# Splitting the remainder weights of a SwiGLU feed-forward part in batches during attention

## The chip, the core and the metric

The kernel runs on one core of a Trainium2 chip. A core has five engines with queues of their own: TensorE (PE, with its weight loads as PEld), VectorE (DVE), ScalarE (ACT), GpSimd (POOL) and SyncE (SP), which here only issues DMAs. ACT issues some DMAs too. Sixteen DMA engines serve all queues. The metric is the device time of one execution in microseconds (us); lower is better.

## What is computed

One transformer block with adaptive layer norm, over 2048 tokens of width 576, all in float32:

```python
mod = silu(c) @ w_mod                      # six rows: sa, ca, ga, sb, cb, gb
h = layernorm(x) * (1 + ca) + sa
x = x + ga * A(h)                          # infini-attention: 32 heads of 18, 4 segments of 512
h = layernorm(x) * (1 + cb) + sb
x = x + gb * ((silu(h @ w_gate) * (h @ w_up)) @ w_down)     # w_gate, w_up: 576 x 4608
```

Attention works segment by segment: softmax over the segment's own 512 keys, mixed with a read of a memory that earlier segments wrote.

## The kernel before

TensorE multiplies in a fast float32 form that drops low bits. To keep precision, an operand is split in two: a high part (ACT casts it) and a low part, the rest (DVE subtracts the high part from the operand). A product is then high x high, low x high and high x low.

**Attention** is one loop over 32 units (four segments with eight groups of four heads) of 11 steps each. In every unit, `p2_step` makes scores (line 599 on PE), their exponential (L602 on ACT) and a causal mask (L606 on POOL); `av_step` (L619) multiplies by the values; `p1_step` (L182, L187) finds the row maxima of a unit two ahead. A table of events (`PAT`) puts the other steps at fixed places of the unit: the output projection `wo_m` (L729) with its DVE addition `wo_x` (L734), the memory read, layer norms. From unit 17 on, `stage_a` and `stage_b` also make part of the feed-forward input; they use the tile `yh12` as scratch. Further work can be hung on step number 11u + k with `at(step, function)`. Each engine runs its instructions in the order in which this loop issues them.

**The feed-forward part** uses Strassen's scheme: seven products in place of eight for the gate and up projections. The features are worked in 18 pairs of blocks of 128 (`p`), each with a gate set and an up set (`z` = 0 and 1), 36 sets in all, and the tokens in two halves (`t`). A half of the width has 288 = 2 x 128 + 32 rows; the 2 x 128 go through the split weights `wh` and `wl` (made by `prep_w`, ACT L1164 and DVE L1165), and the 32 left over, the remainder, go through one product with a tile `wr` (`R[z]`) of 96 used partitions: high part, low part, high part in bands of 32 rows. Four of the seven weight combinations are loaded, three more and a replaced one are sums of these (`sum_o`, L1155). In the first half a set's weights are loaded (`load_o`, tile `O` of 3 x 128 columns, of which the third holds the remainder repeated four times), summed on POOL, and split. The remainder is split by `prep_r`: a cast on ACT (L1149) and a subtraction on DVE (L1150), in two parts of three and four combinations. `store_o` and `store_r` write sums and `wr` to DRAM on ACT's queue, and in the second half they are loaded from there instead.

A pair of blocks has 14 steps `k`; each is one of the seven products for one `z` (seven matmuls at L1200 into banks A, B or C, the last with `wr`), and the down projection of the previous pair lies between them (L1304, L1321). The place of every load, sum and split is written by hand as a condition on `k`. Splits run ahead of their product by `PF` = 5 steps.

Between attention and the first half stands a handover: the last output projections (32 pieces `n`, line 729) run on TensorE, while the first weight sets are loaded, summed (at `n` in `SS`) and split (at `n` in `WW`, DVE's share one piece later through `later` and `flush`) and the rest of the input `y` is made (`y_sum` L1037, `y_here` L1044 and L1046) or loaded (`load_y`, L1122).

Of the kernel before, what the change touches and what calls it, by code (L numbers as in the profile page):

```python
# [7 lines left out]
F32 = mybir.dt.float32  # L8
# [7 lines left out]
P = 128  # L16
# [47 lines left out]
LNA = 1  # L64
S1B, S2B, XB, WB = 2, 2, 2, 1
# [7 lines left out]
def block(ctx: ExitStack, tc: tile.TileContext, x, wqk, wv, wo, beta, wgu, wd, c, w_mod, out):  # L73
# [76 lines left out]
    rD = [[dr.tile([96, 7, P], F32, tag=f"rD{p}_{z}", name=f"rD{p}_{z}") for z in range(2)] for p in range(NF // 2)]  # L150
# [883 lines left out]

    def y_sum(kb):
        n = P if kb < 2 else 96
        nc.gpsimd.tensor_tensor(ys[:n, kb], yh(2, kb)[:n], yh(0, kb)[:n], op=ALU.subtract)  # L1037
# [94 lines left out]
    def load_o(t, p, z):  # L1132
        O[p, z] = o = opl.tile([P, 7, 3, P], F32, tag="O", name="O", bufs=2)
        if t == 0:
            nc.sync.dma_start(o[:, 0:4], wgu[p, z])
        else:
            nc.sync.dma_start(o[:, 0:3, 0:2], wgu[p, z][:, 0:3, 0:2])
            nc.sync.dma_start(o[:, 3:7, 0:2], oD[p][z])

    def store_o(p, z):  # L1140
        nc.scalar.dma_start(oD[p][z], O[p, z][:, 3:7, 0:2])

    def prep_r(t, p, z, part=0):
        r = R[z]
        if t == 1:
            (nc.sync if p or z == 0 else nc.scalar).dma_start(f32(r[0:96]), rD[p][z])
            return
        o, c = O[p, z], slice(0, 3) if part == 0 else slice(3, 7)
        nc.scalar.copy(r[0:96, c], o[0:96, c, 2, :])  # L1149
        later.append(lambda: nc.vector.tensor_tensor(r[32:64, c], o[32:64, c, 2, :], f32(r[32:64, c]), op=ALU.subtract))  # L1150

    def sum_o(p, z, j, eng=nc.gpsimd):
        o = O[p, z]
        d, a, b, op = ((4, 3, 2, ALU.add), (5, 4, 0, ALU.subtract), (3, 0, 3, ALU.subtract), (6, 1, 5, ALU.subtract))[j]
        eng.tensor_tensor(o[:, d], o[:, a], o[:, b], op=op)  # L1155

    def store_r(p, z):
        nc.scalar.dma_start(rD[p][z], f32(R[z][0:96]))

    def prep_w(p, z, m):  # L1160
        o = O[p, z][:, SLOT[m], 0:2]
# [178 lines left out]
    with tc.manual_schedule():  # L1340
# [5 lines left out]
        for u in range(NU + 1):  # L1346
# [38 lines left out]
        load_o(0, 0, 1)  # L1385
        load_y(0, 1)
# [13 lines left out]
        for i in range(4):  # L1400
            for h in range(2):
                for c in range(WC):
# [42 lines left out]
        for t in range(2):  # L1445
            for p in range(NPR):
# [16 lines left out]
                for k in range(14):  # L1463
# [130 lines left out]
def _pairs(*ws):  # L1594
# [5 lines left out]
    r = w[..., 256:, :]  # L1600
    w = np.concatenate([w[..., :256, :], r, r, r, r], axis=-2)
    w = w.reshape(n, len(ws), 2, 2, 3, P, P).transpose(0, 1, 5, 2, 3, 4, 6)
    return np.stack([w[:, :, :, 0, 0], w[:, :, :, 0, 1], w[:, :, :, 1, 1], w[:, :, :, 1, 0]], axis=3)
# [31 lines left out]
```

## Time and profile before

| | |
|---|---|
| median of 3 runs | 1904.1 us (1901.33 to 1904.87) |
| the profiled execution | 1902.24 us |
| its span | 1900.5 us |
| granted TensorE clock, mean | 0.996 |
| instructions | 30716 |
| TensorE, DVE, ACT, POOL busy | 98%, 79%, 49%, 31% |
| DMA traffic | 304.31 MB |

The span runs from the first to the last instruction of the program. Attention runs from 256 to about 615 us of it, the first feed-forward half begins near 642.5 us, the second near 1276 us. In the profile's rows, "out<-in" are the program's tile names, and what stands in brackets is idle time of the engine just before and what ended it. A wait is put down to the engine whose signal came last.

### The profile page before, as it was taken

The numbers are of one execution on the slowest core, as the hardware profiler recorded it, in microseconds if no ns is written. First come the engines' busy times: TensorE is split into PE (matmuls) and PEld (weight loads), VectorE is DVE, ScalarE is ACT, GpSimd is POOL, SyncE is SP. The second block draws the span as 40 slices with busy tenths as digits, with TensorE's granted clock in tenths as the row PEclk, the third lists the DMA queues.
The fourth block names the chain that finished last, engine by engine and source line by source line (L and its number), as shares of the span: only waits on it lengthen the run. The fifth ranks groups of instructions, "written<-read, shape, count | busy, mean of one in ns | idle before, by whom it ended". The sixth has DMA issues, their size and how long they took to land.

```text
span 1900.5 us, 30716 instructions
## 1 busy us (share of the span) xinstructions
PE 1862.9 (98%) x10927; PEld 1559.2 (82%) x10927; DVE 1509.0 (79%) x3277; ACT 933.8 (49%) x2060; POOL 584.4 (31%) x789
## 2 busy tenths in 40 slices
PE   6999999999999899999999999999999999999999
PEld 4888866676766788888888888888888888888888
DVE  6566358878886688898898888876888888888887
ACT  1222267768767444445454454444445454454542
POOL 5212236555556555545544545400000000000000
PEclk9999999999999899999999999999999999999999
DMA  6767555446654854454454454378343233333331
GB/s 190 259 221 249 200 193 155 132 136 175 184 159 127 282 201 160 157 196 158 153 189 158 164 171 149 135 262 257 102 123 104 85 115 102 124 102 101 108 108 59
DMA packets 179424, 304.31 MB, mean 160 GB/s; under 512 B 26152, under 2 KB 107688, under 8 KB 177352
## 3 DMA queue, kind: packets, MB, share of 16 engines
q1 hardware_dynamic: 150696, 245.29, 40.9%
q10 hardware_dynamic: 28576, 57.07, 8.6%
q8 instruction: 86, 1.41, 0.3%
q14 instruction: 66, 0.54, 0.1%
HBM read 187.98 MB, written 113.77 MB: 159 GB/s over the span
## 4 chain that ended last, share of the span: by engine, by line
PE 90%; DVE 3%; DMA 2%; ACT 2%; POOL 1%; issue 1%; SPq 0%; ACTq 0%; DVEq 0%; POOLq 0%
PE A L1200 23%; PE pd L1321 13%; PE C L1200 12%; PE pd L1304 9%; PE B L1200 6%; PE pp L99 6%; PE s L599 4%; PE av L619 4%; PE s L182 4%; PE pv L99 2%; PE pw L729 2%; PE pn L800 1%; PE px L640 1%; ACT Pt L602 1%; PE pm L448 1%
## 5 line engine op out<-in xcount | busy, mean ns | idle before, releaser
L1200 PE MATMUL A<-y,wh 128*128 128x512 f32 x1152 | 404.5, 392 | 1.7 <-ACT B L1246 1.1
L187 DVE CUSTOM_DVE_ANT_0 junk<-s,tri 128x256 bf16<-128x256 f32 (+3 forms) x512 | 228.4, 486 | 68.4 <-PE s L182 60.9
L1165 DVE TENSOR_TENSOR wl<-O,wh 128x256 fp32r<-128x256 f32 x504 | 264.1, 529 | 3.3 <-ACT wh L1164 2.8
L1200 PEld LDWEIGHTS A<-y,wh 128*128 128x128 f32 x1152 | 216.7, 188 | 42.6 <-ACT B L1246 1.7
L1200 PE MATMUL A<-y,wl 128*128 128x512 f32 x576 | 224.8, 390 | 0.0
L602 ACT ACTIVATE Pt<-s 128x512 f32<-128x512 f32 (+1 forms) x352 | 187.9, 559 | 70.2 <-PE s L599 64.4
L1155 POOL TENSOR_TENSOR O<-O 128x384 f32<-128x384 f32 x140 | 158.1, 1142 | 174.3 <-DMA O<-in_wgu_dram 78.8
L1200 PE MATMUL C<-y,wh 128*128 128x512 f32 x576 | 203.6, 394 | 3.8 <-DMA y<-yD 2.5
L1309 DVE TENSOR_TENSOR acc<-acc,pd 128x576 f32<-128x576 f32 x216 | 162.2, 751 | 54.8 <-PE pd L1304 50.6
L1164 ACT CAST wh<-O 128x256 fp32r<-128x256 f32 x504 | 196.9, 405 | 0.8 <-issue 0.7
L1321 PE MATMUL pd<-dh,ah 128*128 128x288 f32 x640 | 189.8, 297 | 0.3 <-DVE acc L1325 0.3
L1321 PE MATMUL pd<-dh,al 128*128 128x288 f32 x640 | 188.2, 294 | 0.0
L1321 PE MATMUL pd<-dl,ah 128*128 128x288 f32 x640 | 188.1, 294 | 0.0
L1325 DVE TENSOR_TENSOR acc<-acc,pd 128x576 f32<-128x576 f32 x156 | 116.7, 749 | 81.8 <-PE pd L1321 81.7
L1264 ACT CAST ah<-sg 128x512 fp32r<-128x512 f32 x192 | 119.3, 621 | 86.1 <-DVE sg L1224 80.4
L599 PE MATMUL s<-qs,ks 110*128 110x512 f32 (+2 forms) x384 | 150.1, 407 | 2.9 <-ACT Pt L602 2.4
L182 PE MATMUL s<-ks,qs 108*128 108x256 f32 (+3 forms) x512 | 140.4, 327 | 1.9 <-DVE mx L187 1.8
L1265 DVE TENSOR_TENSOR al<-sg,ah 128x512 fp32r<-128x512 f32 x192 | 135.6, 707 | 7.1 <-ACT ah L1264 6.8
L1304 PE MATMUL pd<-dh,ah 128*128 128x288 f32 x448 | 132.9, 297 | 0.0
L1304 PE MATMUL pd<-dl,ah 128*128 128x288 f32 x448 | 131.9, 294 | 0.0
L1304 PE MATMUL pd<-dh,al 128*128 128x288 f32 x448 | 131.2, 293 | 0.0
L1200 PEld LDWEIGHTS C<-y,wh 128*128 128x128 f32 x576 | 108.1, 188 | 24.1 <-DMA y<-yD 2.9
(364 smaller groups left out, 4410.9 us busy)
## 6 DMA issues: line engine op xcount, KB each, us to landing
O<-in_wgu_dram SPq DMA_DIRECT2D x36, 768.0 KB
oD<-O ACTq DMA_DIRECT2D x36, 512.0 KB
O<-oD SPq DMA_DIRECT2D x36, 512.0 KB
ks<-kD SPq DMA_DIRECT2D x64, 216.0 KB
qs<-qD SPq DMA_DIRECT2D x64, 216.0 KB
O<-in_wgu_dram SPq DMA_DIRECT2D x36, 384.0 KB
rD<-wr ACTq DMA_DIRECT2D x36, 336.0 KB
wr<-rD SPq DMA_DIRECT2D x35, 336.0 KB
```

What stands on the lines that cost most here:

```text
L99: nc.tensor.matmul(ps, lhsT=a, rhs=b, start=(k == 0), stop=(k == 13))
L182: nc.tensor.matmul(bank[:, n * (h - h0):n * (h - h0) + n], lhsT=qst[b][0:108, h, 128 * i:128 * i + 128], rhs=kst[b][0:108, h // 2, 0:n], s ...
L187: nc.vector.tensor_tensor_reduce(junk[:, :n], bank[:, n * (h - h0):n * (h - h0) + n], tri[:, L - n:], 1.0, -3e38, op0=ALU.add, op1=ALU.max ...
L599: nc.tensor.matmul(bank[:, n * (g - h):n * (g - h + w)].rearrange("p (a b) -> p a b", a=w), lhsT=kst[u % NB][0:110, g // 2, 128 * j:128 * ...
L602: nc.scalar.activation(pt[:, h:h + per, :n], bank[:, :n * per].rearrange("p (a b) -> p a b", a=per), AF.Exp, scale=SCALE)
L1155: eng.tensor_tensor(o[:, d], o[:, a], o[:, b], op=op)
L1164: nc.scalar.copy(wh, o)
L1165: later.append(lambda: nc.vector.tensor_tensor(wl, o, f32(wh), op=ALU.subtract))
L1200: nc.tensor.matmul(bank, lhsT=a, rhs=b, start=(first and n == 0), stop=(n == 6), skip_group_check=not first)
L1304: nc.tensor.matmul(pd[:, i, :288], lhsT=a[:, tk], rhs=w, start=(k == 0), stop=(k == 2))
L1309: nc.vector.tensor_tensor(o, o, pd[:, :, :288], op=ALU.add)
L1321: nc.tensor.matmul(pd[:, i, :288], lhsT=a[:, tk], rhs=w, start=(k == 0), stop=(k == 5))
```

## The change

The remainders of all 36 weight sets are now split in one place, during attention, by a new function `stage_r`. It works in nine batches of four sets, a batch taking two units (22 steps), in units 0 to 17. The host lays the remainders out in a tensor `wgr` of their own, four sets on 4 x 32 = 128 partitions. A batch is: one load on SP (262 KB, 8 steps ahead), four sums on POOL of 128 columns (steps 3 to 6 of the even unit), four casts on ACT of 7 x 32 columns (steps 0 to 3 of the odd unit) with four subtractions on POOL one step later, and two stores on SP of 459 KB (step 8 of the odd unit): the high part and the low part. Scratch is `yh12`, from unit 0 on.

Both halves load `wr` with three DMAs of 32 partitions on SP, high, low, high: `load_r` at steps k = 2 and k = 9, where the second half had one DMA of 96 partitions. `prep_r` and `store_r` are gone. The tile `O` has 2 x 128 columns in place of 3 x 128, its load 512 KB in place of 768 KB in the first half, and `sum_o` 256 columns in place of 384.

```diff
+SUMS = ((4, 3, 2, ALU.add), (5, 4, 0, ALU.subtract), (3, 0, 3, ALU.subtract), (6, 1, 5, ALU.subtract))
...
-    rD = [[dr.tile([96, 7, P], F32, tag=f"rD{p}_{z}", name=f"rD{p}_{z}") for z in range(2)] for p in range(NF // 2)]
+    rD = [[dr.tile([P, 7, P], F32, tag=f"rD{b}_{i}", name=f"rD{b}_{i}") for i in range(2)] for b in range(NF // 4)]
...
+    def stage_r():
+        big = flat(yh12.rearrange("p a b c -> p (a b) c"))
+        ts = [big[:, 896 * i:896 * i + 896].rearrange("p (a b) -> p a b", b=P) for i in range(3)]
+        for b in range(NF // 4):
+            o, h, g = ts[b % 2], ts[2].bitcast(F32R), 22 * b
+            at(max(0, g - 8), lambda b=b, o=o: nc.sync.dma_start(o[:, 0:4], wgr[b]))
+            for j, (d, x_, y_, op) in enumerate(SUMS):
+                at(g + 3 + j, lambda o=o, d=d, x_=x_, y_=y_, op=op: nc.gpsimd.tensor_tensor(o[:, d], o[:, x_], o[:, y_], op=op))
+            for j in range(4):
+                c = slice(32 * j, 32 * j + 32)
+                at(g + 11 + j, lambda o=o, h=h, c=c: nc.scalar.copy(h[:, :, c], o[:, :, c]))
+                at(g + 12 + j, lambda o=o, h=h, c=c: nc.gpsimd.tensor_tensor(o[:, :, c], o[:, :, c], f32(h[:, :, c]), op=ALU.subtract))
+
+            def save(b=b, o=o, h=h):
+                nc.sync.dma_start(rD[b][0], f32(h))
+                nc.sync.dma_start(rD[b][1], o)
+            at(g + 19, save)
...
-        O[p, z] = o = opl.tile([P, 7, 3, P], F32, tag="O", name="O", bufs=2)
+        O[p, z] = o = opl.tile([P, 7, 2, P], F32, tag="O", name="O", bufs=2)
...
-        o, c = O[p, z], slice(0, 3) if part == 0 else slice(3, 7)
-        nc.scalar.copy(r[0:96, c], o[0:96, c, 2, :])
-        later.append(lambda: nc.vector.tensor_tensor(r[32:64, c], o[32:64, c, 2, :], f32(r[32:64, c]), op=ALU.subtract))
...
+    def load_r(p, z):
+        b, g = divmod(2 * p + z, 4)
+        for i in range(3):
+            nc.sync.dma_start(f32(R[z][32 * i:32 * i + 32]), rD[b][i % 2][32 * g:32 * g + 32])
...
+                if u == 0 and k == 0:
+                    stage_r()
...
         load_o(0, 0, 1)
+        load_r(0, 0)
         load_y(0, 1)
...
                     if n in WW:
-                        j = WW.index(n)
-                        if j < 2:
-                            prep_r(0, 0, 0, j)
                         prep_w(0, 0, next(gw))
...
-                    if t:
-                        if k == 2 + swap:
-                            prep_r(1, p, 1)
-                        elif not last and k == 9:
-                            prep_r(1, nx, 0)
-                    else:
-                        if k in (3, 5):
-                            prep_r(0, p, 1, k // 5)
-                        elif tn == 0 and k in (9, 10):
-                            prep_r(0, nx, 0, k - 9)
-                        elif tn and k == 8:
-                            prep_r(1, 0, 0)
+                    if k == 2 + swap:
+                        load_r(p, 1)
+                    elif not last and k == 9:
+                        load_r(nx, 0)
+                    if t == 0:
...
-                        elif k == 3:
-                            store_r(p, 0)
-                        elif k == 8:
-                            store_r(p, 1)
```

More of the change, by code (lines that the diff above doesn't have):

```diff
@@ L72, in block @@
 @with_exitstack
-def block(ctx: ExitStack, tc: tile.TileContext, x, wqk, wv, wo, beta, wgu, wd, c, w_mod, out):
+def block(ctx: ExitStack, tc: tile.TileContext, x, wqk, wv, wo, beta, wgu, wgr, wd, c, w_mod, out):
     nc = tc.nc
@@ L1136, in load_o @@
         else:
-            nc.sync.dma_start(o[:, 0:3, 0:2], wgu[p, z][:, 0:3, 0:2])
-            nc.sync.dma_start(o[:, 3:7, 0:2], oD[p][z])
+            nc.sync.dma_start(o[:, 0:3], wgu[p, z][:, 0:3])
+            nc.sync.dma_start(o[:, 3:7], oD[p][z])
     def store_o(p, z):
[L1141 to L1147, printed above, removed]
-        o, c = O[p, z], slice(0, 3) if part == 0 else slice(3, 7)
-        nc.scalar.copy(r[0:96, c], o[0:96, c, 2, :])
-        later.append(lambda: nc.vector.tensor_tensor(r[32:64, c], o[32:64, c, 2, :], f32(r[32:64, c]), op=ALU.subtract))
+        nc.scalar.dma_start(oD[p][z], O[p, z][:, 3:7])
+    def load_r(p, z):
+        b, g = divmod(2 * p + z, 4)
+        for i in range(3):
+            nc.sync.dma_start(f32(R[z][32 * i:32 * i + 32]), rD[b][i % 2][32 * g:32 * g + 32])
     def sum_o(p, z, j, eng=nc.gpsimd):
         o = O[p, z]
-        d, a, b, op = ((4, 3, 2, ALU.add), (5, 4, 0, ALU.subtract), (3, 0, 3, ALU.subtract), (6, 1, 5, ALU.subtract))[j]
+        d, a, b, op = SUMS[j]
         eng.tensor_tensor(o[:, d], o[:, a], o[:, b], op=op)
-    def store_r(p, z):
-        nc.scalar.dma_start(rD[p][z], f32(R[z][0:96]))
     def prep_w(p, z, m):
-        o = O[p, z][:, SLOT[m], 0:2]
+        o = O[p, z][:, SLOT[m]]
         wh = wp.tile([P, 2, P], F32R, tag="wh", name="wh")
```

12 lines of the change are left out of this document (7 added, 5 removed).

## The prediction

> **What bounds the kernel now.** I read the page first (engine shares, the chain that ended last), then a table of the span by stretches of 100 us, then TensorE's waits around the change from attention to the feed-forward part, then the order of time there.
>
> ```profile
> span 1900.5 us, 30716 instructions
> PE 1862.9 (98%) x10927; PEld 1559.2 (82%) x10927; DVE 1509.0 (79%) x3277; ACT 933.8 (49%) x2060; POOL 584.4 (31%) x789
> PE 90%; DVE 3%; DMA 2%; ACT 2%; POOL 1%; issue 1%; SPq 0%; ACTq 0%; DVEq 0%; POOLq 0%
> ```
>
> TensorE is busy for 98% of the span and holds 90% of the chain. So an instruction taken from another engine counts only where TensorE waits for it. The table by stages tells where that is (columns: PE, PEld, DVE, ACT, POOL busy, granted clock, DMA share, GB/s):
>
> ```profile
> 300.00:400.00 100.00, 99.83 (x735) 68.20 (x734) 82.80 (x345) 75.94 (x155) 55.94 (x111) 1.00 0.47 140
> 600.00:700.00 100.00, 88.97 (x516) 73.36 (x514) 69.87 (x117) 50.85 (x112) 52.96 (x55) 0.95 0.65 225
> 800.00:900.00 100.00, 100.00 (x556) 88.66 (x555) 87.03 (x130) 49.89 (x117) 47.73 (x44) 1.00 0.53 177
> 1500.00:1600.00 100.00, 100.00 (x545) 87.95 (x544) 86.69 (x162) 48.68 (x114) 0.00 (x0) 1.00 0.34 107
> ```
>
> Both feed-forward halves (800 and 1500) leave TensorE no idle time; POOL's work in the first half is hidden. Attention (300) is at 99.83, but ACT at 76 and DVE at 83 are close behind it. Only the handover, 600 to 700, is loose: 11 us idle, clock 0.95. TensorE's waits there:
>
> ```profile
> PE pw L729 <- DVE xr L734: 4.4, 2, 4.1
> PE C L1200 <- DMA y<-yD: 2.5, 1, 2.5
> PE C L1200 <- DVE cu L1223: 1.3, 1, 1.3
> PE A L1200 <- ACT B L1246: 1.1, 1, 1.1
> ```
>
> **The change part by part. A, the 4.1 us wait.** In order of time:
>
> ```profile
> 618.27 3.82 POOL L1037 TENSOR_TENSOR ys<-yh,yh 128x512 f32<-128x512 f32 x3
> 623.85 1.48 POOL L1155 TENSOR_TENSOR O<-O 128x384 f32<-128x384 f32 x1
> 626.41 1.00 POOL L1155 TENSOR_TENSOR O<-O 128x384 f32<-128x384 f32 x1
> 630.60 0.99 POOL L1155 TENSOR_TENSOR O<-O 128x384 f32<-128x384 f32 x1
> 631.62 0.62 ACT L1149 CAST wr<-O 96x512 fp32r<-96x512 f32 x1 [5.97 <-POOL O L1155]
> 632.27 0.68 DVE L1150 TENSOR_TENSOR wr<-O,wr 32x512 fp32r<-32x512 f32 x1 [4.21 <-ACT wr L1149]
> 633.93 0.45 DVE L734 TENSOR_TENSOR xr<-pw,xr 128x288 f32<-128x288 f32 x1
> 634.43 0.61 PE L729 MATMUL pw<-woh,oh 128*128 128x288 f32 x1 [4.14 <-DVE xr L734]
> 634.84 0.44 PE L729 MATMUL pw<-wol,oh 128*128 128x288 f32 x1
> 640.65 0.30 PE L729 MATMUL pw<-woh,oh 128*128 128x288 f32 x1
> 640.79 0.29 PE L729 MATMUL pw<-wol,oh 128*128 128x288 f32 x1
> ```
>
> Between 618 and 632 POOL works without a break through three y sums, two memsets and four weight sums with memsets between. ACT stands 5.97 us on the second part of the remainder split (wr), which needs all four sums; DVE stands behind ACT, and its addition that frees the output projection's PSUM bank stands behind wr on DVE. The change deletes wr from ACT and DVE. ACT's next need of POOL is then the wh cast for m = 6, which needs two sums, ended by about 626.6 (623.85, two sums, one memset of 0.95), and its DVE half stands after that addition, not ahead of it. So the addition comes when TensorE does: 4.14 us go. The 28 matmuls that follow (634.43 to 640.65) took 6.22 us; at the spacing of the last two rows (0.14, 28 x 0.133 = 3.7) they are 2.5 shorter. A = -6.6; the end that is certain not to be exceeded is -6.9 with the 0.26 us of the same pair's other wait, the other end 0, if another ACT or DVE step is late in its place. I take -6.6, since DVE stood idle for 4.21 us ahead of wr, so nothing else was waiting there to be late.
>
> The Trainium skill, "TensorE: Matmul & The Clock Gate", Part 1, says that the clock falls to half after an idle window of about 3.4 us. The trace agrees for the 4.14 us wait, less for the next one, 2.52 us, which is also followed by a slow stretch (0.83 below); by the rule alone the upper end of B would be 2.5 instead of 4.2.
>
> **B and C, the waits after it.**
>
> ```profile
> 650.00:660.00 10.00, 7.48 (x26) 5.94 (x26) 7.21 (x11) 4.99 (x12) 4.58 (x6) 0.83 1.01 343
> 644.81 0.43 SPq L1122 DMA_DIRECT2D y<-yD  x1
> 652.59 0.50 PE L1200 MATMUL C<-y,wh 128*128 128x512 f32 x1 [2.52 <-DMA y<-yD]
> 653.17 0.34 SPq L1135 DMA_DIRECT2D O<-in_wgu_dram  x1
> 658.68 4.55 POOL L1155 TENSOR_TENSOR O<-O 128x384 f32<-128x384 f32 x4 [5.18 <-DMA acc<-xD]
> 658.87 0.39 PE L1200 MATMUL A<-y,wr 128*128 128x512 f32 x1
> 671.64 0.50 PE L1200 MATMUL C<-y,wh 128*128 128x512 f32 x1 [1.27 <-DVE cu L1223]
> 671.87 0.52 ACTq L1141 DMA_DIRECT2D oD<-O  x1
> 674.57 0.50 PE L1200 MATMUL A<-y,wh 128*128 128x512 f32 x1 [1.05 <-ACT B L1246]
> ```
>
> B: the y load that TensorE waits for is issued behind the output projection's last store on SP, so it moves up with A and the wait stays. The DMA engines are full there (1.01). The R store of 336 KB leaves, three R loads of 112 KB come. These loads for set (0,1) stand on SP behind the O load of 653.17; the first matmul that reads that set's R is at 658.87, 5.7 us after. The O load itself was usable 5.5 us after its issue (POOL, 658.68). Its bytes fall from 768 to 512 KB, R adds 336, so R lands about when it is needed. Best end: wait and slow clock go, -2.5 - 10 x 0.17 = -4.2. Worst end: R comes 2.5 us late and the clock falls again, as after 2.52: +4.2. I take 0, between nearly equal ends.
>
> One more order changes on SP: the R load of set (0,0) goes to a buffer that lay under attention's tiles and waits, as the changed program has it, for POOL's last attention addition, which ends where the y sums begin (618.27); the loads of y behind it on SP are held up to then. Their first readers come some 20 us later: 0, and 1 us if the full DMA engines pass the delay on.
>
> C: the waits of 1.27 and 1.05 come from DVE steps stretched beside POOL's sums and from ACT's store that stands until the sums end (671.87). The sums shrink from 384 to 256 columns (below: 1142 to about 786 ns, four times 0.36) and two wr steps leave DVE: 1.4 us and more, so most goes. -2.0 (ends 0 and -2.3).
>
> **D, the halves.** First half: 140 sums get 0.36 us shorter (50 us of POOL), wr leaves ACT and DVE, the R stores leave ACT's queue, O loads lose a third of their bytes, three R loads per set come on SP. TensorE is at 100.00 there: 0; without that cover it would be those 50 us, and the 0.3 that the table lacks of 400 is the most. R loads are issued when the last reader of that buffer is done, five steps ahead of the next. Second half: three loads for one on SP, same places: 0, as POOL and ACT show no part in it. What is queued behind them on SP (O, wd) has the rest of a pair of feature blocks.
>
> **E, attention.** Nine batches, each four sums of 128 columns, four casts and four subtractions of 224, one load, two stores.
>
> ```profile
> L815 POOL TENSOR_TENSOR nm<-nm 128x76 f32<-128x76 f32 x12 | 4.2, 348 | 0.2
> L1025 POOL TENSOR_TENSOR yh<-yh 128x256 f32<-128x256 f32 x4 | 3.1, 786 | 0.0
> L1155 POOL TENSOR_TENSOR O<-O 128x384 f32<-128x384 f32 x140 | 158.1, 1142 | 174.3 <-DMA O<-in_wgu_dram 78.8
> L606 POOL TENSOR_SCALAR_AFFINE_SELECT Pt<-Pt 128x512 f32<-128x512 f32 x128 | 83.0, 658 | 101.7 <-ACT Pt L602 101.3
> L1164 ACT CAST wh<-O 128x256 fp32r<-128x256 f32 x504 | 196.9, 405 | 0.8 <-issue 0.7
> L599 PEld LDWEIGHTS s<-qs,ks 110*128 110x128 f32 x365 | 67.1, 190 | 48.9 <-ACT Pt L602 33.1 <-ACT qe L778 6.7 <-ACT nm L809 4.8
> 439.50:450.40 10.90, 10.90 (x83) 7.35 (x79) 10.04 (x44) 8.81 (x18) 4.21 (x10) 1.00 0.48 156
> 462.00:473.60 11.60, 11.60 (x87) 7.71 (x84) 10.05 (x47) 10.40 (x21) 4.48 (x10) 1.00 0.77 229
> ```
>
> POOL: between 348 ns for 76 and 786 for 256 columns, 128 cost about 0.475 and 224 about 0.71: 36 x 0.475 + 36 x 0.71 = 42.6 us. POOL stands 101.7 us ahead of its 128 masks waiting for ACT, 3.2 us a unit, 57 us in the 18 units: it fits. In each step the mask is queued before the new work, and its reader on TensorE comes some three steps later: 0 (up to +3, if a mask is late once in most batches).
>
> ACT: 36 casts of 224 columns at 405 x 224/256 = 0.35 to 0.40, 13.6 us, in the steps 0 to 3 of every odd unit, each between two exponentials. TensorE's weight loads already stand 33.1 us for those exponentials, so this is not free. How much lands on the path: the last two rows are odd units of the same kind, the second with the y transform's steps added. ACT rises by 1.59 us, the unit by 0.70, in which four matmuls more lie: at most 0.44 a microsecond, about 0.3 with the matmuls taken out. +4.0; ends 0 and +13.6. DMA: 1.18 MB in two units, at a share of 0.47: 0. SP issues 27 more, all with a unit or more to spare; the first use of the y buffer at unit 0 stands behind nothing that is late.
>
> **Sum**: -6.6 + 0 - 2.0 + 0 + 4.0 = -4.6. The profiled execution took 1902.24 (span 1900.5 and 1.7 around it), the median shown is 1904.1; I count from halfway, 1903.2: **1898.6 us**.
>
> **The rivals.** *Slower: ACT sets the pace in attention.* Every cast lies on the path, as each exponential in steps 0 to 3 waits for a cast and TensorE for the exponential's bank: -6.6 - 2.0 + 13.6 = +5.0, 1908.2. For it: the 33.1 us. Against: units with more ACT work grew by less than half of it. It decides from 63% of the casts' time (8.6 of 13.6).
>
> *No change: the R load takes the wait over.* B at its worst end and a little of C lost: -4.6 + 4.2 + 0.8 = +0.4, 1903.6. For it: 5.5 against 5.7 us, at full DMA engines. Against: the bytes ahead of it are fewer. The Trainium skill, "DMA: Bandwidth & Descriptors", Rules for kernel authors, advises one 128-partition transfer over several on part of the partitions, as these share the same engines; that speaks against three loads for one, and no run here shows it yet.
>
> *More: the whole handover closes up* and attention hides the casts: -6.6 - 4.2 - 2.3 = -13.1, 1890.1. For it: y's load has 336 KB less beside it. Against: it still stands behind the store.
>
> **How the numbers follow.** Forecast 0.46 (own range 1895 to 1902), more 0.17, R late 0.13, ACT 0.24. The range goes from 1889, a microsecond beyond the case of more, to 1911, which is the slower case with the 3 us that a late mask may add. What can be told from no change is 0.2%, 3.8 us: below 1900.3 or above 1907.9. Faster: three quarters of the forecast's 0.46, and 0.17: 0.52. Slower: 0.24, the case of ACT, alone or with late masks. Same: the rest, 0.24.
>
> **What would show it.** A: no TensorE wait over 1 us for xr, granted clock 1.00 between 630 and 640 us, the output projection's end some 7 us earlier against attention's end. B: the wait for y or one for wr ahead of the first A with wr. C: no waits of cu and B about 30 us after. D: both halves at 100.00, equal lengths. E: odd units 1 to 17 longer by about 0.45 us, POOL masks ahead of their readers. I am wrong if the units grow by 1 us and more, or if a half shows waits for wr.

## The result and the profile after

The changed kernel takes 1908.27 us (median of 12 runs), the kernel before 1903.78 beside it: ratio 1.0028, interval 1.0018 to 1.0038. It is slower by about 5 us, where 1898.6 was forecast. The profiled execution has a span of 1906.3 us, 5.8 more than the 1900.5 of before. The head of the page after, and its line of the chain by engine:

```profile
span 1906.3 us, 30956 instructions
PE 1863.4 (98%) x10927; PEld 1558.9 (82%) x10927; DVE 1413.2 (74%) x3205; ACT 910.2 (48%) x2024; POOL 567.5 (30%) x861
PE 89%; DMA 4%; ACT 3%; DVE 2%; POOL 2%; issue 1%; SPq 0%; ACTq 0%; DVEq 0%; POOLq 0%
```

DVE, ACT and POOL together have 136 us less work and the kernel is slower: outside the handover that work did not lie on the path. What grew most on the chain is DMA, from 2% to 4%. The same stretches as before (columns as there):

```profile
300.00:400.00 100.00, 99.13 (x723) 65.89 (x723) 82.82 (x338) 79.60 (x174) 72.60 (x142) 0.99 0.59 185
600.00:700.00 100.00, 92.93 (x573) 75.00 (x566) 61.66 (x132) 52.67 (x116) 52.62 (x66) 0.98 0.70 221
800.00:900.00 100.00, 100.00 (x556) 88.70 (x556) 71.05 (x117) 44.51 (x105) 39.79 (x45) 1.00 0.52 164
1500.00:1600.00 100.00, 100.00 (x545) 87.95 (x544) 86.71 (x161) 49.05 (x114) 0.00 (x0) 1.00 0.35 108
```

The handover (600) has less idle time, the middle of both halves none, as before. TensorE's waits after, over the whole span (us in total, times, longest):

```profile
PE s L600 <- ACT Pt L603: 6.7, 12, 1.3
PE C L1212 <- DMA y<-yD: 4.7, 1, 4.7
PE A L1212 <- DMA wr<-rD: 4.1, 1, 4.1
PE s L600 <- DMA qs<-mr: 2.0, 1, 2.0
```

The wait for xr is gone. The wait for wr is new; those for y (2.5 before), for qs (0.4) and for Pt (2.4 in total, 0.6 at most) have grown. Where they lie follows from the starts of TensorE's instructions, counted in products (seven matmuls each, so every stage is cut at the same instruction in every kernel):

| stage, us | before | after |
|---|---|---|
| start to the first score | 256.20 | 255.61 |
| attention, to its last product with the values | 358.33 | 367.05 |
| handover, to the first product A | 27.98 | 20.68 |
| first half | 633.21 | 631.88 |
| second half, to its last product | 607.58 | 613.60 |
| to the end of the span | 17.2 | 17.5 |

So the handover gained 7.3 us, and attention lost 8.7 and the second half 6.0. Both losses sit in few places. Of the 18 pairs of blocks of the second half, 17 agree to 0.01 us (33.59 each in most of them); the first took 36.01 us before and 42.03 after. Of attention's units these changed (from one unit's first score of 512 columns to the next one's):

| unit | 1 | 3 and 4 | 9 | 11 | 13 and 15 | 17 | 18 |
|---|---|---|---|---|---|---|---|
| before | 9.48 | 20.22 | 10.67 | 10.90 | 23.85 | 10.90 | 11.55 |
| after | 10.00 | 24.59 | 10.88 | 11.36 | 26.54 | 11.39 | 11.61 |

**Half boundary.** SP's queue and TensorE, after, in order of time; then the one R load of that place before:

```profile
1279.54 0.37 SPq L1142 DMA_DIRECT2D y<-yD  x1
1284.44 3.97 SPq L1165 DMA_DIRECT2D wr<-rD  x3
1297.06 0.50 PE L1212 MATMUL A<-y,wr 128*128 128x512 f32 x1 [4.05 <-DMA wr<-rD]
```
```profile
1290.00:1300.00 10.00, 5.95 (x33) 5.32 (x32) 1.09 (x2) 2.20 (x6) 0.00 (x0) 0.89 0.88 274
```
```profile
1280.69 0.31 ACTq L1146 DMA_DIRECT2D wr<-rD  x1
```

Before, this load alone stood on ACT's queue and was issued at 1280.69. Now three stand on SP behind loads of y and O, and are issued from 1284.44 to 1288.1. TensorE waits 4.05 us and runs slower for some us after (clock 0.89).

**Units 13 and 15.** POOL and ACT after, then ACT's same step before:

```profile
403.24 0.67 POOL L1047 TENSOR_TENSOR yh<-yh 128x224 f32<-128x224 f32 x1
403.86 0.64 POOL L607 TENSOR_SCALAR_AFFINE_SELECT Pt<-Pt 128x512 f32<-128x512 f32 x1
404.47 1.29 POOL L1047 TENSOR_TENSOR yh<-yh 128x224 f32<-128x224 f32 x2
405.73 0.27 POOL L761 TENSOR_SCALAR nb<-mv,rs 128x1 f32<-128x1 f32 x1
406.04 0.87 ACT L762 ACTIVATE xh<-xr,nb,rs 128x576 f32<-128x576 f32 x1 [2.38 <-POOL nb L761]
```
```profile
399.27 0.87 ACT L761 ACTIVATE xh<-xr,nb,rs 128x576 f32<-128x576 f32 x1 [0.50 <-POOL nb L760]
```

Three subtractions stand on POOL ahead of `nb`, a step of 0.27 us of the layer norm. ACT waits 2.38 us for it, with the next exponentials queued behind, and TensorE 1.29 us for these.

**Units 3 and 4.** A piece of the chain and TensorE's row behind it, after and then before:

```profile
291.13 6.21 DMA qs<-mr
297.48 0.57 PE L600 MATMUL s<-qs,ks 110*128 110x512 f32 x1 [1.98 <-DMA qs<-mr]
```
```profile
290.65 4.73 DMA qs<-mr
295.52 0.47 PE L599 MATMUL s<-qs,ks 110*128 110x512 f32 x1 [0.35 <-DMA qs<-mr]
```

This DMA brings 8 KB, the negative row maxima of the next unit. It was issued 0.5 us later and took 1.5 us longer; TensorE waits 1.98 us for it in place of 0.35, and the clock is below 1.00 for some 10 us after:

```profile
295.00:300.00 5.00, 3.02 (x20) 1.22 (x12) 2.74 (x13) 1.79 (x4) 3.59 (x6) 0.77 0.94 330
300.00:305.00 5.00, 5.00 (x35) 2.66 (x31) 3.21 (x14) 3.72 (x9) 1.96 (x5) 0.89 0.54 167
```

### The profile page after: what moved, and what is told of

Same layout as the page of the kernel before. It is cut to its first block, busy times and chain, and to the rows that moved or that the text cites. A ratio compares the mean times of both kernels' runs of the same rounds, so it can differ in the third digit from the quotient of the medians.

```text
span 1906.3 us, 30956 instructions
## 1 busy us (share of the span) xinstructions
PE 1863.4 (98%) x10927; PEld 1558.9 (82%) x10927; DVE 1413.2 (74%) x3205; ACT 910.2 (48%) x2024; POOL 567.5 (30%) x861
## 4 chain that ended last, share of the span: by engine, by line
PE 89%; DMA 4%; ACT 3%; DVE 2%; POOL 2%; issue 1%; SPq 0%; ACTq 0%; DVEq 0%; POOLq 0%
PE A L1212 24%; PE pd L1333 13%; PE C L1212 12%; PE pd L1316 9%; PE B L1212 6%; PE pp L100 5%; PE s L600 4%; PE av L620 4%; PE s L183 3%; PE pv L100 3%; PE pw L730 2%; DMA y<-yD 1%; ACT Pt L603 1%; PE pn L801 1%; DMA O<-in_wgu_dram 1%
## 5 line engine op out<-in xcount | busy, mean ns | idle before, releaser
L1177 DVE TENSOR_TENSOR wl<-O,wh 128x256 fp32r<-128x256 f32 x504 | 240.1, 482 | 3.3 <-ACT wh L1176 2.9
L1170 POOL TENSOR_TENSOR O<-O 128x256 f32<-128x256 f32 x140 | 111.6, 810 | 179.3 <-DMA O<-in_wgu_dram 82.2
```

Source lines behind the costliest of these rows:

```text
L1177: later.append(lambda: nc.vector.tensor_tensor(wl, o, f32(wh), op=ALU.subtract))
```

## Experiments

Each row of times below is compared with the changed kernel's (or a variant's) own stages; ratios are against the kernel before. Stage times come from one profile per run, and the kernel before has one. Most units and pairs repeat within 0.05 us where an edit does not touch them. Of those named here these do not: the first pair of the first half (27.98 to 29.91 us in nine runs with the changed kernel's handover), the first pair of the second half (42.03 to 44.02 in eight that left it alone), unit 18 (11.61 to 13.07) and units 3 and 4 together (22.44 to 25.16 in five that left both alone).

**Handover: what removed the wait for xr?** The split was put back, into a tile that nobody reads.

```diff
+                        if WW.index(n) < 2:
+                            c = slice(0, 3) if n == WW[0] else slice(3, 7)
+                            o = O[0, 0]
+                            nc.scalar.copy(rx[0:96, c], o[0:96, c, 1, :])
+                            later.append(lambda c=c, o=o: nc.vector.tensor_tensor(
+                                rx[32:64, c], o[32:64, c, 1, :], f32(rx[32:64, c]), op=ALU.subtract))
                         prep_w(0, 0, next(gw))
```

> In the handover the two-part split of a remainder is put back on ACT and DVE at its old places, into a tile that nobody reads, from the columns that are there. Theory A of the prediction (ACT stands on the four sums with this cast, DVE behind it, and the addition that frees the output projection's bank behind that): a wait for xr of 3 us or more comes back, with the sums now 0.36 us shorter about 1.4 us less than the old 4.14, and the stretch from attention's end to the first product grows from 20.7 us by 4 to 6. Rival 'shorter sums and less on DVE': the stretch grows by under 1.5 us, as the wait went because the sums got shorter.

1913.4 us (one run); the handover takes 26.17 us in place of 20.68, +5.5. ACT, DVE and TensorE:

```profile
637.89 0.62 ACT L1435 CAST rx<-O 96x512 fp32r<-96x512 f32 x1 [5.04 <-POOL O L1170]
638.54 0.68 DVE L1436 TENSOR_TENSOR rx<-O,rx 32x512 fp32r<-32x512 f32 x1 [3.67 <-ACT rx L1435]
640.70 0.40 PE L730 MATMUL pw<-woh,oh 128*128 128x288 f32 x1 [3.60 <-DVE xr L735]
```

The same chain as before the change, link by link, with the shorter sums in place. So 5.5 of the 7.3 us are the two steps that stood in line; the other 1.8 go with the rest (shorter sums and lighter loads), which no run separates further.

**Half boundary: the queue, the place, or three DMAs for one?** First the three DMAs on ACT's queue, then on SP one step earlier.

```diff
-    def load_r(p, z):
+    def load_r(p, z, eng=nc.sync):
...
-            nc.sync.dma_start(f32(R[z][32 * i:32 * i + 32]), rD[b][i % 2][32 * g:32 * g + 32])
+            eng.dma_start(f32(R[z][32 * i:32 * i + 32]), rD[b][i % 2][32 * g:32 * g + 32])
...
-                        load_r(p, 1)
+                        load_r(p, 1, nc.scalar if swap else nc.sync)
```

> The one R load of the half boundary (three DMAs) goes to ACT's queue, where the kernel before had its one DMA; everything else as in the changed kernel. Theory 'SP's order': the second half grew by 6.0 us because the three DMAs stand on SP behind loads that cannot start yet; then TensorE's wait for wr (4.05 us) is gone, the second half falls from 613.6 to about 607.6 us and the time from 1908.3 to about 1902.3. Rival 'three for one': three DMAs of 32 partitions are slow at full DMA engines on any queue; then a wait for wr of 2 us or more stays and the time is 1906 or more.

```diff
+                    if swap and k == 2:
+                        load_r(p, 1)
...
-                    if k == 2 + swap:
+                    if k == 2 and not swap:
```

> The same three DMAs stay on SP but are put one step earlier, ahead of the two O loads. 'SP's order' in its narrow form (they are late because of the two O loads issued just ahead, and of what DMA time these take): the wait for wr shrinks from 4.05 to under 1 us and the second half falls by 5 to 6 us, as in the run with ACT's queue. Form 'SP stands as a whole': SP itself is held by earlier y loads, so the three DMAs issue less than 1 us earlier than 1284.4 and the wait stays above 2 us. 'Three for one': the wait stays at about 4 us whatever the place.

On ACT: 1905.28 us, ratio 1.0008 (0.9998 to 1.0019); the second half 609.28, the first pair 37.72; the time lies between the theory's 1902.3 and the rival's 1906. On SP, earlier: 1906.15, ratio 1.0011 (1.0001 to 1.0021); the pair still 41.17. TensorE's wait in each, that of ACT's queue first:

```profile
1291.43 0.47 PE L1212 MATMUL A<-y,wh 128*128 128x512 f32 x1 [1.55 <-DMA y<-yD]
```
```profile
1293.96 0.58 PE L1212 MATMUL A<-y,wr 128*128 128x512 f32 x1 [2.42 <-DMA wr<-rD]
```

Three DMAs for one are not slow as such: from ACT's queue all three are there in time. On SP they are late because SP issues them late. In the changed kernel the three issues begin 9.2, 10.0 and 12.9 us after the half's first product. SP's waits ahead of them (us in total, times, longest), and the chain:

```profile
SPq L1165 <- DMA y<-yD: 5.5, 3, 2.6
```
```profile
1278.12 9.97 DMA y<-yD
1288.10 8.91 DMA wr<-rD
```

The third R load is issued when a y load has landed that has nothing to do with it, and so are the other two. The traces show why: eight completion semaphores serve the DMAs of both queues in turn, and a DMA is issued only when the one that had its semaphore before has landed. On ACT's queue the three are issued 5.0, 5.4 and 5.9 us after the half's first product, since the DMAs that had their semaphores before had landed. There a y load on SP stands 5.5 us until the first of them has landed (1288.9), and TensorE waits 1.55 us for an earlier y load: one late load is exchanged for another. ACT's row, and the chain ahead of TensorE's wait:

```profile
1281.97 1.30 ACTq L1165 DMA_DIRECT2D wr<-rD  x3
```
```profile
1280.34 10.96 DMA y<-yD
```

One step earlier on SP the issues begin at 6.2, 7.0 and 9.9 us, 3.0 earlier, each again just behind a landing of y, and the wait falls to 2.42. That is the form 'SP stands as a whole': the y loads hold the three, and not only the O loads, at a DMA share of 1.02 to 1.03. No run put one DMA of 96 partitions on SP. The third of the three is issued 3.7 us after the first, so that three for one can have cost a large part of the wait there. The Trainium skill, "DMA: Bandwidth & Descriptors", Queues, rings and completion order, says that SP and ACT have one ring each on each of the same 16 DMA engines, that descriptors are taken in ring order and that an engine goes round its rings packet by packet. The run with ACT's queue agrees: of the three, issued 1.6 us and more after that y load, the first two landed at 1288.9 and 1290.1, the y load at 1291.3. How much of the gain that is stays open, since on ACT the three were also issued 4 to 7 us earlier.

**Units 13 and 15: POOL's order or ACT's casts?**

```diff
-                at(g + 12 + j, lambda o=o, h=h, c=c: nc.gpsimd.tensor_tensor(o[:, :, c], o[:, :, c], f32(h[:, :, c]), op=ALU.subtract))
+                at(g + 17 + j // 2, lambda o=o, h=h, c=c: nc.gpsimd.tensor_tensor(o[:, :, c], o[:, :, c], f32(h[:, :, c]), op=ALU.subtract))
...
-            at(g + 19, save)
+            at(g + 20, save)
```

> The four subtractions on POOL in each odd unit go from steps 1 to 4 to steps 6 and 7, behind layer norm's small POOL step nb, and the two stores one step later. Theory 'POOL ahead of nb': units 13 and 15 (13.28 and 13.26 us) fall back to about 11.9 each, ACT's idle time of 2.38 us ahead of xh falls to 0.5, and attention is 2.7 us shorter; the casts stay and so do the 0.2 to 0.5 us of units 1, 9, 11 and 17. Rival 'casts' (the ACT rival of the prediction): all odd units keep their length within 0.3 us, since the casts stand where they stood.

Units 13 and 15 are 11.91 and 11.94, exactly as before the change, with all casts in place. But the time is 1909.03 (ratio 1.0027, 1.0016 to 1.0038): units 6 (10.98), 9 (11.57), 11 (11.60) and 17 (11.63) grew, by 1.8 us together, and unit 18 (12.70) by 1.1 as in other runs that left the subtractions alone. The expectation that the rest stays as it was is wrong. In unit 9 two subtractions are now ahead of a mask:

```profile
360.41 1.29 POOL L1047 TENSOR_TENSOR yh<-yh 128x224 f32<-128x224 f32 x2
361.65 0.64 POOL L607 TENSOR_SCALAR_AFFINE_SELECT Pt<-Pt 128x512 f32<-128x512 f32 x1
362.34 0.85 PE L620 MATMUL av<-Pt,vq 128*32 128x384 f32 x8 [0.62 <-POOL Pt L607]
```

POOL has idle time in every unit, and still neither place tried is free for all nine batches: each has a small step of another chain close behind.

**What do the casts cost?** They were left out (`nc.scalar.copy` deleted, its output set to zero once), and in a second run moved to steps 5 to 8, with the subtractions in steps 6 to 9.

> The 36 casts on ACT in attention are left out (the high part stays zero, so both feed-forward halves compute with wrong remainders); loads, sums, subtractions and stores stay. Forecast's price for the casts: units 1 to 17 together 4 us shorter, spread evenly, 0.45 us an odd unit. Rival of the prediction ('ACT sets the pace'): 8.6 us or more, all odd units. Theory after the earlier runs ('POOL ahead of nb, bytes ahead of qs'): only the 0.2 to 0.5 us of units 1, 9, 11 and 17 go (about 1.7 us), units 13 and 15 keep at least 12.7 us since the subtractions still stand ahead of nb, and units 3 and 4 keep a wait for qs.

> The changed kernel with the casts of every odd unit in steps 5 to 8 in place of 0 to 3, the subtractions in steps 6 to 9, the stores at step 10. If the casts cost because they stand ahead of the exponentials and of the copy mr early in the unit, units 1, 9, 11 and 17 fall to 9.5, 10.7, 10.9 and 10.9 (1.6 us less), 13 and 15 to 11.9 (2.7 less), and mr is issued 0.64 us earlier; units 3 and 4 keep a wait for qs if the bytes do that. If a cast costs wherever it stands, the odd units keep their length and only 13 and 15 fall. Masks late by the subtractions, as when these stood in steps 6 and 7, would add up to 0.7 us in units 6, 9, 11 or 17.

Without casts, units 1, 9, 11 and 17 are 9.47, 10.78, 11.08 and 11.11: 1.2 us less, of the 1.7 that these had grown. Units 13 and 15 stay at 13.27 and 13.25, units 3 and 4 at 26.29. In unit 3 a wait of TensorE of 0.62 us for an exponential goes with the casts. So they cost 1.2 us in those four units and at most 0.6 in unit 3, not 4 and not 13.6. And the small DMA qs<-mr, issued as early in unit 3 as before the change (5.02 us into it, 5.07 before, 5.72 with the casts), was still waited for, 2.39 us: the lateness of mr alone does not make it late. Later in the unit they are no cheaper: units 1, 9, 11 and 17 are 10.27, 10.92, 11.42 and 11.58, unit 2 is 11.65 and unit 6 11.25, and only 13 and 15 are back at 11.91 and 11.94, since the subtractions stand behind `nb` there too. One run each: 1910.46 and 1911.24 us.

**Units 3 and 4: why is a DMA of 8 KB late?** Four edits of what shares SP's queue with it: the batch's load two steps later (behind it), six steps earlier (in the unit before; this one is part of the larger run below), the stores of batch 1 taken out of the unit, and the small DMAs on ACT's queue.

```diff
-            at(max(0, g - 8), lambda b=b, o=o: nc.sync.dma_start(o[:, 0:4], wgr[b]))
+            at(max(0, g - 6), lambda b=b, o=o: nc.sync.dma_start(o[:, 0:4], wgr[b]))
```

> Each batch's load goes from step 3 to step 5 of the odd unit before it, which is behind the small DMA qs<-mr on SP. Theory 'bytes ahead of qs': unit 3 (12.07) and unit 4 (12.52) fall back to about 10 and 10.3 us, the wait of 2.0 us for qs is gone, attention is about 4.3 us shorter. Rival 'mr late': the casts on ACT make the copy mr 0.5 us late and that alone sets it; then unit 3 keeps at least 11.5 us and unit 4 at least 12. Third possibility, 'stores': the two stores of 459 KB fill the DMA engines and the wait moves to them; units 3 and 4 keep half or more of their growth.

```diff
-                nc.sync.dma_start(rD[b][0], f32(h))
-                nc.sync.dma_start(rD[b][1], o)
+                for d in {1: (), 4: (4, 1)}.get(b, (b,)):
+                    nc.sync.dma_start(rD[d][0], f32(h))
+                    nc.sync.dma_start(rD[d][1], o)
```

> Batch 1 does not store in unit 3; its place is filled in unit 9, where batch 4's result is stored twice (so four weight sets of the halves get wrong remainders). Theory 'bytes beside qs': units 3 and 4 fall from 24.6 us together (22.4 at the least in the runs so far) to 20.7 or less, near the 20.22 of the kernel before; in unit 9, where the bytes double, the unit grows only if a small DMA is waited for there. Rival 'mr late by the casts': units 3 and 4 stay above 22.

```diff
-            nc.sync.dma_start(f32(qst[b][108 + a:109 + a]).rearrange("p a t -> p (a t)"), mr[16 * a:16 * a + 16])
+            (nc.scalar if u == 4 else nc.sync).dma_start(f32(qst[b][108 + a:109 + a]).rearrange("p a t -> p (a t)"), mr[16 * a:16 * a + 16])
```

> The changed kernel with only the two small DMAs qs<-mr of unit 3 (for unit 4) issued on ACT's queue, not SP's; all bytes as in the changed kernel. If they land late because they stand in SP's queue behind larger loads, they land within 4.5 us of their issue, the wait of 2 us goes and units 3 and 4 fall to about 21 together, less than 1 us of it given back for two issues on ACT. If it is the fullness of the DMA engines, whoever issues, the wait stays above 1 us and units 3 and 4 above 22.

| | after | load behind it | no stores | load one unit earlier | on ACT |
|---|---|---|---|---|---|
| wait for qs, us | 1.98 | 1.03 | 1.90 | 0.47 | none |
| units 3 and 4, us | 24.59 | 22.32 | 23.09 | 21.62 | 27.20 |

Without the stores the wait is the same: they come behind it. With the load moved behind it the wait is 1.03 us, with the load in another unit 0.47. The chain with the load one unit earlier, 4.72 us, as before the change:

```profile
287.87 4.72 DMA qs<-mr
```

Eight runs that left the load at its place (the changed kernel among them) had waits of 1.00 to 2.39 us, so the first of these moves, with 1.03, proves little; the second, 0.47 and no wait at all in a repeat below, lies outside that. The run with the casts later had no wait for qs here but one of 1.4 us a unit earlier. So the load's 256 KB ahead of it in SP's queue are the likeliest cause of most of the 4.4 us, by runs that scatter. A part of the scatter, and about 1.5 of the 4.4 us (12.52 in unit 4, for 11.0 where the clock stays up), is the clock behind the wait (last section). Unit 4 keeps at least 0.7 us (11.0 for 10.29) in every run; POOL is busy without a break there, the sums among it, but no run took them out of that unit, and it stays open. On ACT the small DMA is not waited for, but ACT is, for its issue. ACT's row, and the chain there:

```profile
287.36 3.75 ACTq L171 DMA_DIRECT2D qs<-mr  x2
291.15 0.87 ACT L603 ACTIVATE Pt<-s 128x384 f32<-128x384 f32 x2 [3.82 <-DMA qs<-qD]
```
```profile
283.55 7.03 DMA qs<-qD
290.60 0.51 ACTq L171
```

The second of the two issues stands until a load issued on SP 3.8 us earlier has landed: it had the same one of the eight semaphores, as at the half boundary. On ACT that cost 3.75 us of exponentials, and unit 3 was 16.16 us. The ratios and times: load behind it 1910.82, ratio 1.0030 (1.0017 to 1.0042); one run each of no stores 1910.85 and ACT 1909.38. None of the three pays.

**Together.** Three edits, then five, then six, each for a place found above.

```diff
-        for z in range(2):
+        for z in range(3):
             R[z] = wrp.tile([P, 7, P], F32R, tag=f"wr{z}", name="wr")
...
-    def load_r(p, z):
+    def load_r(p, z, to=None):
...
-            nc.sync.dma_start(f32(R[z][32 * i:32 * i + 32]), rD[b][i % 2][32 * g:32 * g + 32])
+            nc.sync.dma_start(f32(R[z if to is None else to][32 * i:32 * i + 32]), rD[b][i % 2][32 * g:32 * g + 32])
...
-                    if k == 2 + swap:
+                    if swap and k == 2:
+                        R[1] = R[2]
+                    elif k == 2:
                         load_r(p, 1)
+                    elif t == 0 and p == NPR - 1 and k == 5:
+                        load_r(0, 1, 2)
...
-                at(g + 12 + j, lambda o=o, h=h, c=c: nc.gpsimd.tensor_tensor(o[:, :, c], o[:, :, c], f32(h[:, :, c]), op=ALU.subtract))
+                at(g + (17 + j // 2 if b in (6, 7) else 12 + j), lambda o=o, h=h, c=c: nc.gpsimd.tensor_tensor(o[:, :, c], o[:, :, c], f32(h[:, :, c]), op=ALU.subtract))
-            at(g + 19, save)
+            at(g + (20 if b in (6, 7) else 19), save)
...
         load_y(0, 5)
+        load_y(0, 3)
...
         load_d(0, 0)
-        load_y(0, 3)
```

> Three edits of the changed kernel at three separate places. Half boundary: the R of the second half's first up set goes to a third tile, loaded seven steps earlier in the last pair of the first half; by 'the R load is late' the first pair of the second half falls from 42.0 us to 36 or less, by 'full DMA engines' the wait moves to y and the pair stays above 38. Attention: the subtractions of batches 6 and 7 alone stand behind nb; units 13 and 15 at 11.9 and the rest unchanged, 2.7 us less. Handover: the load of y's fourth operand is issued ahead of the output projection's last four stores; the 4.7 us wait for y and the slow clock behind it go, 4 to 6 us less from the first product to the second pair, or, if the DMA engines are the limit, the wait moves to another operand. All right: about 1908 - 6 - 2.7 - 5 = 1894 us; the rivals together: above 1904.

```diff
         load_r(0, 0)
+        load_r(0, 1)
...
-                    elif k == 2:
+                    elif k == 2 and (t or p):
                         load_r(p, 1)
...
-            at(max(0, g - 8), lambda b=b, o=o: nc.sync.dma_start(o[:, 0:4], wgr[b]))
+            at(max(0, g - 14), lambda b=b, o=o: nc.sync.dma_start(o[:, 0:4], wgr[b]))
```

> The three edits of the run before, and two more. Handover: the R of the second weight set is loaded together with the first set's, some 25 us before it is needed; by 'the wait went on to R because its load stands behind the O load' the 3.51 us wait for wr goes and the first pair falls from 28.65 to about 24 us; by 'the DMA engines are the limit' another wait of 2 us or more appears in it and it stays above 27. Attention: each batch's load goes six steps further forward, into the even unit before, away from the unit in which segment 1's values are loaded. If the load's bytes are what makes the small DMA qs<-mr late, units 3 and 4 together fall from 24.6 to 20.5; if the stores do it or nothing in particular, they stay above 22. Sum: 1896.7 - 4.5 - 4 = 1888 at best, 1896.7 if the rivals hold.

```diff
+            def save_h(b=b, h=h):
+                nc.sync.dma_start(rD[b][0], f32(h))
+            if b == 8:
+                at(g + 15, save_h)
...
-                nc.sync.dma_start(rD[b][0], f32(h))
+                if b < 8:
+                    nc.sync.dma_start(rD[b][0], f32(h))
```

> The five edits of the run before, and the last batch's high part stored four steps earlier (step 4 of unit 17, not 8). In unit 18 stage_a loads into scratch that lies over this high part, and its load waits for the store; eleven runs of the changed kernel and its variants gave unit 18 between 11.61 and 13.07 us against 11.55 before, the long ones with a wait of 0.6 us for the small DMA qs<-mr. If the store's lateness and the bytes bunched behind it do that, unit 18 is under 11.8 us and the time about 1894.7; if not, it stays near 12.7 and the time at 1895.7. By five rounds the whole should stand 0.4 to 0.55% below the kernel before.

| us | after | three | five | six |
|---|---|---|---|---|
| median | 1908.27 | 1896.70 | 1895.72 | 1894.69 |
| ratio to before | 1.0028 | 0.9964 | 0.9952 | 0.9951 |
| its interval | 1.0018 to 1.0038 | 0.9950 to 0.9977 | 0.9936 to 0.9969 | 0.9937 to 0.9965 |
| units 3 and 4 | 24.59 | 24.59 | 21.62 | 21.05 |
| units 13 and 15 | 26.54 | 23.85 | 23.85 | 23.85 |
| unit 18 | 11.61 | 12.74 | 12.75 | 11.55 |
| first pair, first half | 29.91 | 28.65 | 25.35 | 24.96 |
| first pair, second half | 42.03 | 37.31 | 35.89 | 36.29 |

Units 13 and 15 behave as the theory had it. The half boundary comes to 37.31 us, between the theory's 36 and the rival's 38. The handover does not gain: with y's fourth operand loaded early, the wait moved to the R load that stands behind an O load, and 28.65 us lies within the scatter. TensorE's row, then two pieces of the chain: that R load is issued when a store of O on ACT's queue has landed.

```profile
657.51 0.61 PE L1212 MATMUL A<-y,wr 128*128 128x512 f32 x1 [3.51 <-DMA wr<-rD]
```
```profile
644.27 7.38 DMA oD<-O
651.67 0.33 SPq L1165
```

With that load taken forward too, the pair falls by another 3.3 us, and no wait in it is longer than 0.82. But the second pair gives back 1.5 us (36.55 for 35.04), since two waits of before are back:

```profile
PE C L1212 <- DVE cu L1235: 0.8, 1, 0.8
PE A L1212 <- ACT B L1258: 1.1, 1, 1.1
```

Units 3 and 4 come to 21.62, where the theory had 20.5 and the rivals over 22. The time fell by 1.0 us, not by the 8.5 hoped for, and the intervals of the three versions overlap, so what the fourth to sixth edit are worth shows in the stages alone. The first pair of the second half comes back to the 36.01 of before once R is out of the crowd. The last edit took unit 18 back to 11.55: its load into scratch no longer waits for a late store; one profile each, beside 11.61 to 13.07 in the other runs of the changed kernel and its variants. The version with six edits computes the whole block and takes 8.8 us less than the kernel before, 13.6 less than the changed kernel.

## Why the prediction was wrong

Against the forecast of -4.6 us the span grew by 5.8. Both signs of being wrong that the prediction named came: units that grew by over 1 us, and a wait for wr in a half. The terms, in us of the profiled executions:

| step | forecast | measured |
|---|---|---|
| A, the handover | -6.6 | -7.3 |
| B and C, the two first pairs | -2.0 | -0.5 |
| D, the first half's other pairs | 0 | -0.8 |
| D, the second half | 0 | +6.0 |
| E, attention | +4.0 | +8.7 |
| before attention and after the last product | not in the sum | -0.3 |

**A was right**, in size and by its chain: with the split put back, 5.5 us of it return. DVE and ACT had nothing else late there, as the 4.21 and 5.97 us of idle time ahead of wr had said.

**B was taken at 0, and that holds within the scatter.** In this profile the wait stayed with y, not with R, and grew from 2.52 to 4.73 us; the first pair grew by 0.8, since C's wait of 1.27 us at its end is gone. In the nine runs with this handover the wait for y was 3.03 to 4.73 us, and the first pair 27.98 to 29.91, for 29.12 before. The step "it moves up with A and the wait stays" held in six of the nine: the two y loads are issued 2.0 to 2.3 and 2.5 to 2.8 us after the first product, for 2.3 and 2.8 before. In the changed kernel's profile the load moved up less than A did. A piece of the chain, then the rows:

```profile
636.49 9.79 DMA xD<-xr
```
```profile
646.29 1.08 SPq L1141 DMA_DIRECT2D y<-yD  x1
647.41 1.73 SPq L1142 DMA_DIRECT2D y<-yD  x1
655.62 0.50 PE L1212 MATMUL C<-y,wh 128*128 128x512 f32 x1 [4.73 <-DMA y<-yD]
```

The first product came 7.3 us earlier after attention's end, and the y loads were issued 3.0 and 4.1 us after that product, the first of them when a store of the output projection, issued 9.8 us earlier, had landed. They then shared full DMA engines (1.03 from 650 to 660). Why the wait is over 2.52 us in the other six runs too stays open. What the wait was worth showed only when both late loads went: 25.35 us, of which the next pair gives back 1.5.

**C came out right, but not by the shorter steps alone**: the waits of 1.27 and 1.05 are gone and the second pair is 1.3 us shorter; with B that gives the -0.5. In the two runs in which neither y nor R is late, a wait of 0.8 us for cu and one of 1.1 for B are back, and the second pair takes 36.55 us, for 36.52 before the change. So the shorter steps and the late y seem to have done it together.

**D, first half: right.** DVE's 87 fell to 71 and POOL's 48 to 40 at no gain, since TensorE was at 100.00 in both.

**D, second half: the step that failed**, and the larger part of the error: "three loads for one on SP, same places: 0". The places are the same in the program, the queue is not. One load of the 36, at the half boundary, stood on ACT's queue, in the row quoted above and in `prep_r`, which goes (`nc.sync if p or z == 0 else nc.scalar`). I looked at the middle of the halves, where TensorE never waits, and took the boundary for granted. On SP the loads were issued 9.2 to 12.9 us after the half's first product, where ACT had issued its one at 5.0, and TensorE waited 4.05 us. The other 35 loads were worth nothing, as forecast. The rival "the R load takes the wait over" had the mechanism, R late at full DMA engines, at the wrong place and too cheap (4.2 us); three DMAs for one, for which it named a rule against them, are not slow as such; what one DMA on SP would have cost stays open.

**E: the sum was half of what it cost, and for another reason.** POOL's and ACT's durations came out as estimated (0.46 us for the sums, then the subtractions and the casts):

```profile
L1047 POOL TENSOR_TENSOR yh<-yh 128x224 f32<-128x224 f32 x36 | 23.6, 668 | 0.9 <-ACT yh L1046 0.5
L1046 ACT CAST yh<-yh 128x224 fp32r<-128x224 f32 x36 | 13.6, 378 | 0.1
```

But the casts, priced at 4.0, cost 1.2 to 1.8. "It fits: 0" for POOL failed at units 13 and 15 (2.7 us): 57 us of slack over 18 units say nothing of the one place where three subtractions of 0.67 us stand ahead of a step of 0.27 us that ACT waits for. I looked at the masks alone, and not at the layer norm's step. "DMA: 0, at a share of 0.47" failed at units 3 and 4 (4.4 us, of which 1.6 are the longer wait for qs, about 1.5 the slow clock behind it, 0.7 what unit 4 keeps, the rest the wait behind the casts): the mean hides that 256 KB stand ahead of a small DMA with a deadline, in the unit where other loads meet. That these bytes are the cause is likely, not shown.

The rival "ACT sets the pace" gave 1908.2 us, and 1908.27 was measured. That is luck, and the rival was still false: with every cast left out attention took 368.84 us, no less than the 367.05 with them.

## What to carry to other kernels

Work that is moved into idle time is paid where it enters a queue: for each place look for the next small instruction or small DMA behind it that another engine waits for, not at the engine's share. In a diff, read the queue of every DMA that is replaced, above all the exceptional ones at a boundary, since an exception written by hand can mark a place where the common queue is late, as here. For a load that lands late, look first when it was issued and what its issue stood for: here it was, at two places, an unrelated DMA that had the same completion semaphore, and three DMAs for one take three of the eight. When a change removes buffers, spend the room on loading early what is read at a crowded boundary: a third tile of 3.5 KB per partition took 4.7 to 6.1 us from that pair here.

## What the runs showed of the hardware

A wait of 1.6 to 2.4 us can halve TensorE's clock, or not. Behind waits of 1.62 to 2.39 us for qs<-mr it fell in five runs, and unit 4 took 12.26 to 14.37 us; behind 1.90 and 2.15 us in two others it stayed at 1.00, and unit 4 took 11.01 and 11.06. After a wait of 1.73 us (the run with R on ACT's queue) and of 1.90 us (the run without the stores), in windows of the same place (the second wait ends in its window, and the clock stays at 1.00 to 315 us):

```profile
300.00:305.00 5.00, 5.00 (x26) 2.60 (x26) 2.31 (x9) 2.64 (x5) 0.44 (x1) 0.51 0.62 182
```
```profile
300.00:305.00 5.00, 4.75 (x35) 2.99 (x35) 3.23 (x11) 3.58 (x8) 2.42 (x5) 1.00 0.70 205
```

The Trainium skill, "TensorE: Matmul & The Clock Gate", Part 1, says that the gate looks at free-running windows of about 3.4 us; that a shorter wait counts or not by where it falls would agree, but no run here moved a wait within its window.

A DMA of 8 KB took 4.7 to 7.2 us from issue to landing (7.20 in unit 18 of the run with three edits), most likely by what was issued ahead of it. And a DMA issue can hold the issuing engine until an unrelated DMA that had its semaphore has landed: ACT for 3.75 us, for a DMA of another queue (7.03 us in flight), SP for 5.5 us ahead of three loads. Then whatever stands behind it on that engine waits too.
